# A kernel with a static order: the scheduler may now pick the engine of many operations and ranks by the following chain, and loads, stores and tables are rearranged

## The chip, the cores and the metric

The kernel runs on one core of a Trainium2 chip. The metric is the device time in microseconds (us) of one execution, and the medians below are over the executions of one kernel. On the core, TensorE (PE in the profile, with its weight loads as PEld) does the matrix products; VectorE (DVE), ScalarE (ACT) and GpSimd (POOL) do the elementwise work; SyncE (SP) issues most of the transfers.

## The reference

For 4 batches and 8 heads, with 768 steps and 40 channels per head, a recurrence (RWKV-7) updates a 40x40 state. The 8 heads' outputs, side by side, are a 768x320 matrix per batch. It is mixed by a Fourier transform over the sequence and over the model dimension, added to itself, layer-normalised and sent through an MLP.

```python
for t in range(S):                               # S = 768; per batch and head
    y[:, :, t] = einsum('bhd,bhde->bhe', r_t, state)
    Sa = einsum('bhde,bhe->bhd', state, a_t)
    state = state * w_t - einsum('bhd,bhe->bhde', Sa, b_t) + einsum('bhd,bhe->bhde', v_t, k_t)
x = y.transpose(0, 2, 1, 3).reshape(B, S, 320)
mixed = real(fft(fft(x, axis=1), axis=2))
u = x + mixed
un = (u - mean(u)) / sqrt(var(u) + 1e-6)         # per row of 320
out = u + maximum(un @ w_ch1, 0) @ w_ch2         # 320 -> 1280 -> 320
```

## The kernel before

The kernel works in 24 chunks of 128 steps, six per batch. For each chunk there is a preparation (loads, logarithms, products with the decay, transposes, masked 128x128 products) and a chain that carries the state from chunk to chunk. The last instruction of the chain is the DVE multiply that writes the chunk's output; where I give the time of "the chunk's output" it is the start of this multiply, which lasts 0.5 us. After the sixth chunk of a batch follow mixing, normalisation and MLP of that batch, and they overlap with the next batch's chunks. Only the last batch's have nothing to overlap with.

The program first lists its operations in Python, each with its engine, an assumed duration and what it reads and writes. A list scheduler then turns this into one fixed order per engine, which the chip executes in order:

```python
# class Plan, cut
def op(self, eng, occ, fn, w=(), r=(), lat=None, ...):
    o.eng, o.occ, o.fn, o.prio = eng, occ, fn, self.prio      # one engine, one assumed duration
    ...
def run(self, log=None):
    while left:
        for e in self.ENG:
            ...                                               # start time of each ready operation
            t0 = min(c[0] for c in cand)
            t, _, o = min((c for c in cand if c[0] <= t0 + self.slack), key=lambda c: (c[1], c[0]))
            ...                                               # lowest prio (= program step) first
        o.fn()                                                # emits the instruction
```

The parts that the argument touches are the masks (A, N, RV and M are the four masked products of a chunk), the layer normalisation between mixing and MLP, the store of the residual (x, to which the mix is added) and the loads of the MLP weights:

```python
# masks of A and N: on DVE, per half; of RV and M: two copies on ACT and one select on POOL
op("DVE", DVE(512), lambda ...: nc.vector.tensor_tensor(dst()[:, e], p2[e](), msk, Alu.mult), ...)
...
op("ACT", ACT(512), lambda ...: nc.scalar.copy(RV()[:, e], p2[e]()), ...)
op("POOL", 1.06, lambda: causal(RV()), w=[RV])

# layer normalisation; st holds mean and variance of three tiles of 128 rows
op("DVE", 0.12, eps, w=[st], r=[])                             # variance + 1e-6
op("POOL", 0.25, lambda st=st: nc.gpsimd.tensor_tensor(st()[:, 8:11], st()[:, 8:11], mhalf, Alu.pow), w=[st])
for ti in range(3):
    op("DVE", 0.45, lambda ...: nc.vector.tensor_scalar(
        un()[:, ti], u()[:, ti], st()[:, 2 * ti:2 * ti + 1], st()[:, 8 + ti:9 + ti],
        Alu.subtract, Alu.mult), w=[un[ti]], r=[u[ti], st])    # (u - mean) * (1/sigma), written as bf16
# then: transposes of un on PE, unT to SBUF by ACT, MLP products on PE

# residual: one store of the batch's six chunks (960 KB) after the last one
op("SP", 0.9, lambda: nc.sync.dma_start(xd().rearrange("(c t) d -> t c d", t=C), xb()), w=[xd], r=[xb], lat=6.0)
```

I call the DVE instruction that writes `un` "the normalisation". There are 24 of them: two halves of three tiles in each of four batches.

## Time and profile before

| what | before |
|---|---|
| median of three runs | 326.75 us (326.4 to 328.29) |
| span of the profiled run | 324.8 us |
| busy PE / DVE / ACT / POOL | 284.0 / 218.4 / 199.1 / 193.5 us |
| sixth output (end of the first batch's recurrence) | 91.9 us |
| last output (24th), and from it to the end | 286.75 us, 38.1 us |

From the page of the kernel before come the rows that matter of the busy tenths (40 equal slices of the span, so about 8.1 us each; a digit is the busy share in tenths, and PEclk is the granted TensorE clock in tenths of full speed), the shares of the chain that ended last by engine, and two groups. A group's columns are line, engine, operation, tiles, shapes and count, then busy us and mean ns of one, then idle time before it.

```profile
PE   6649875768899989999999999999997899978995
POOL 8947999653699744744896555657764642252100
PEclk9985999676999999999999999999999999999999
...
PE 47%; DVE 14%; ACT 6%; POOL 5%; issue 5%; DVEq 0%; ACTq 0%; POOLq 0%
...
L545 DVE TENSOR_SCALAR un_192<-u_175,sm_213 128x320 bf16<-128x320 f32 x6 | 3.4, 600 | 0.4 <-POOL sm_213 L543 0.4
L629 POOL TENSOR_SCALAR u_177<-u_177,sm_213 128x320 f32<-128x320 f32 x2 | 1.0, 530 | 0.0
```

PE is near its limit in the middle and is not in the first quarter, where its clock is also granted at 0.5 to 0.7 for some slices. The second group, L629, is a piece of the table generation on POOL: a multiply by a per-partition scalar and an addition of a constant, 530 ns.

The stretches view divides the span at the ends of the sixth and of the last output's multiply. Its columns are the stretch, its length, then the busy us of each engine with its count of instructions, the granted clock, the busy share of the DMA engines, and GB/s.

```profile
core 0: us, PE busy (x) PEld busy (x) DVE busy (x) ACT busy (x) POOL busy (x), PEclk, DMA share, GB/s
0.00:92.40 92.40, 68.29 (x979) 47.08 (x980) 65.85 (x111) 49.28 (x112) 69.86 (x111) 0.85 0.89 148
92.40:287.20 194.80, 184.41 (x2752) 136.06 (x2750) 140.46 (x287) 134.75 (x322) 117.38 (x160) 1.00 0.50 108
287.20:324.80 37.60, 31.25 (x223) 20.81 (x221) 12.11 (x33) 15.07 (x34) 6.22 (x12) 1.00 0.24 80
```

The middle keeps PE busy for 184.41 of 194.80 us, or 95%, at full clock. The head keeps it busy for 74%. A part of this is filler: where the scheduler foresees a gap on PE it emits products of a constant tile. The trace has 60 of them (18.8 us of PE, most of it in head and tail), so PE's busy times are not all useful work.

The timeline view has start us, duration us, engine, line, operation, tiles, shapes and count; in brackets stand the engine's idle time before it and what ended it. Here are the first two products with the decay on POOL, and the last batch's normalisation:

```profile
10.19 0.86 POOL L330 TENSOR_TENSOR nat_90<-in_117,rw_138 128x320 bf16<-128x320 f32 x1
20.56 0.86 POOL L330 TENSOR_TENSOR nat_91<-in_124,rw_139 128x320 bf16<-128x320 f32 x1 [3.91 <-DMA in_124<-in_b_dram]
...
298.36 0.87 POOL L543 TENSOR_TENSOR sm_215<-sm_215,mhalf 128x3 f32<-128x3 f32 x1 [3.69 <-DVE sm_215 L541]
299.37 1.13 DVE L545 TENSOR_SCALAR un_191<-u_176,sm_215 128x320 bf16<-128x320 f32 x3
299.83 0.17 PEld L557 LDWEIGHTS <-un_191 128*128 128x128 bf16 x3 [1.84 <-DVE un_191 L545]
301.62 0.65 PE L278 MATMUL ps_220<-unT_193,w1sb 128*128 128x384 bf16 x3 [0.31 <-ACT unT_193 L559]
```

### The profile page before, as it was taken

How to read it: one execution, taken by the hardware profiler on the slowest of the kernel's cores; microseconds unless marked ns; L12 is line 12 of the kernel's file. 1: busy time of each engine (PE TensorE's matmuls, PEld its weight loads, DVE VectorE, ACT ScalarE, POOL GpSimd, SP SyncE). 2: the span in 40 equal slices, each digit the busy share in tenths (PEclk: the TensorE clock that was granted, in tenths of full speed). 3: DMA queues.
4: the chain of work that ended last, by engine and by line, in shares of the span. 5: the costliest groups of instructions: out<-in, count | busy, mean ns of one | idle time of the engine just before them, and what ended most of it. 6: DMA issues, size and time to landing. Idle time of an engine off the chain costs nothing.

```text
span 324.8 us, 9858 instructions
## 1 busy us (share of the span) xinstructions
PE 284.0 (87%) x3948; PEld 203.9 (63%) x3948; DVE 218.4 (67%) x429; ACT 199.1 (61%) x468; POOL 193.5 (60%) x282
## 2 busy tenths in 40 slices
PE   6649875768899989999999999999997899978995
PEld 2438653555568765777787667767775566655663
DVE  7246799993977898675489996637769973306411
ACT  2225753477588478496767684975763895531850
POOL 8947999653699744744896555657764642252100
PEclk9985999676999999999999999999999999999999
DMA  8999999972788955456599763539300001134011
GB/s 137 189 169 185 171 167 169 177 124 42 122 202 197 156 97 89 91 109 128 162 194 183 130 110 89 107 77 242 123 4 2 0 2 64 42 141 124 0 61 63
DMA packets 161518, 37.67 MB, mean 116 GB/s; under 512 B 150656, under 2 KB 161152, under 8 KB 161472
## 3 DMA queue, kind: packets, MB, share of 16 engines
q1 hardware_dynamic: 159808, 35.40, 54.3%
q0 software_dynamic: 1664, 1.64, 3.0%
q8 instruction: 31, 0.51, 0.6%
q14 instruction: 15, 0.12, 0.1%
HBM read 30.80 MB, written 7.86 MB: 119 GB/s over the span
## 4 chain that ended last, share of the span: by engine, by line
PE 47%; DVE 14%; ACT 6%; POOL 5%; issue 5%; DVEq 0%; ACTq 0%; POOLq 0%
PE ps_219 L278 6%; PE ps_226 L278 5%; PE ps_223 L278 5%; PE ps_224 L278 4%; PE ps_220 L278 4%; PE ps_221 L278 3%; PE ps_222 L278 3%; PE ps_225 L278 3%; DVE un_191 L545 1%; PE ps_222 L294 1%; PE ps_225 L294 1%; DVE un_192 L545 1%; PE ps_221 L294 1%; PE ps_223 L294 1%; DVE pr_163 L367 1%
## 5 line engine op out<-in xcount | busy, mean ns | idle before, releaser
L278 PEld LDWEIGHTS <-w1sb 128*128 128x128 bf16 x240 | 21.5, 97 | 13.9 <-issue 1.2
L302 POOL TENSOR_SCALAR_AFFINE_SELECT pr_161<-pr_161 128x1024 bf16<-128x1024 bf16 x8 | 8.9, 1119 | 22.6 <-ACT pr_161 L431 12.0
L302 POOL TENSOR_SCALAR_AFFINE_SELECT pr_160<-pr_160 128x1024 bf16<-128x1024 bf16 x7 | 7.7, 1097 | 11.3 <-ACT pr_160 L431 10.1
L458 POOL TENSOR_TENSOR pm_173<-xb_172 128x320 bf16<-128x320 f32 x12 | 10.1, 861 | 3.2 <-DVE xb_172 L444 3.1
L458 POOL TENSOR_TENSOR pm_174<-xb_171 128x320 bf16<-128x320 f32 x12 | 10.1, 857 | 2.5 <-DVE xb_171 L444 2.4
L349 PEld LDWEIGHTS <-nat_91 128*128 128x128 bf16 x96 | 6.4, 105 | 8.2 <-POOL nat_91 L330 7.4
L302 POOL TENSOR_SCALAR_AFFINE_SELECT pr_159<-pr_159 128x1024 bf16<-128x1024 bf16 x6 | 7.3, 1214 | 6.8 <-ACT pr_159 L431 6.7
L302 POOL TENSOR_SCALAR_AFFINE_SELECT pr_164<-pr_164 128x1024 bf16<-128x1024 bf16 x7 | 7.7, 1095 | 4.6 <-ACT pr_164 L372 2.9
L349 PEld LDWEIGHTS <-nat_90 128*128 128x128 bf16 x96 | 6.1, 103 | 6.2 <-POOL nat_90 L330 5.6
L302 POOL TENSOR_SCALAR_AFFINE_SELECT pr_166<-pr_166 128x1024 bf16<-128x1024 bf16 x7 | 7.7, 1097 | 3.7 <-ACT pr_166 L372 2.4
L278 PEld LDWEIGHTS <-pm_174 128*128 128x128 bf16 x72 | 6.7, 110 | 2.6 <-POOL pm_174 L458 1.2
L260 PEld LDWEIGHTS <-ident_71 128*128 128x128 bf16 x60 | 5.4, 108 | 4.0 <-POOL ident_71 masks.py:199 2.0
L349 PEld LDWEIGHTS <-nat_92 128*128 128x128 bf16 x96 | 6.7, 109 | 1.7 <-POOL nat_92 L330 0.9
L278 PEld LDWEIGHTS <-pr_161 128*128 128x128 bf16 x136 | 5.5, 98 | 3.3 <-issue 1.4
L278 PEld LDWEIGHTS <-pr_159 128*128 128x128 bf16 x128 | 5.0, 97 | 3.7 <-POOL pr_159 L302 1.7
L294 PEld LDWEIGHTS <-kb_151 64*128 64x128 bf16 x128 | 4.3, 98 | 4.4 <-issue 3.3
L278 PEld LDWEIGHTS <-pm_173 128*128 128x128 bf16 x72 | 6.3, 108 | 0.8 <-issue 0.2
L349 PEld LDWEIGHTS <-nat_93 128*128 128x128 bf16 x96 | 6.2, 100 | 0.8 <-POOL nat_93 L330 0.5
L543 POOL TENSOR_TENSOR sm_213<-sm_213,mhalf 128x3 f32<-128x3 f32 x4 | 3.4, 853 | 5.6 <-DVE sm_213 L541 5.4
L302 POOL TENSOR_SCALAR_AFFINE_SELECT pr_163<-pr_163 128x1024 bf16<-128x1024 bf16 x5 | 5.5, 1094 | 2.0 <-ACT pr_163 L431 1.8
L278 PEld LDWEIGHTS <-pr_165 128*128 128x128 bf16 x128 | 5.3, 98 | 2.0 <-DVE pr_165 L367 0.7
L543 POOL TENSOR_TENSOR sm_215<-sm_215,mhalf 128x3 f32<-128x3 f32 x4 | 3.5, 873 | 5.1 <-DVE sm_215 L541 4.9
(1338 smaller groups left out, 1188.4 us busy)
## 6 DMA issues: line engine op xcount, KB each, us to landing
xd<-xb_172 SPq DMA_DIRECT2D x2, 960.0 KB, 4.9
xd<-xb_171 SPq DMA_DIRECT2D x2, 960.0 KB, 4.4
out_dram<-ot_210 SPq DMA_DIRECT2D x8, 160.0 KB, 1.8
out_dram<-ot_211 SPq DMA_DIRECT2D x8, 160.0 KB, 1.9
out_dram<-ot_212 SPq DMA_DIRECT2D x8, 160.0 KB, 1.8
u_178<-xd SPq DMA_DIRECT2D x6, 160.0 KB, 4.0
u_175<-xd SPq DMA_DIRECT2D x6, 160.0 KB, 4.0
u_176<-xd SPq DMA_DIRECT2D x6, 160.0 KB, 3.0
```

The source lines that it names most:

```text
L260: nc.tensor.matmul(ps.tiles[i][:, :m_], ident16, fill16[:, :m_], start=True, stop=True)
L278: nc.tensor.matmul(o, l_, r_, start=first, stop=True, skip_group_check=True)
L294: nc.tensor.matmul(ps2[e]()[:, q, :], lT[e * 64:(e + 1) * 64, q, :], rT[e * 64:(e + 1) * 64, q, :], start=(q == 0), stop=True, skip_group_ ...
L302: nc.gpsimd.affine_select(out=t_, in_=t_, compare_op=Alu.is_gt, fill=0.0, base=0, pattern=[[0, 2], [0, NP], [1, 128]], channel_multiplier=-1)
L349: nc.tensor.transpose(pt()[:, x_, q, :], nt()[:, j, 2 * q:2 * q + 2, :].rearrange("t h d -> t (h d)"), ident16)
L367: op("DVE", DVE(512), lambda dst=dst, p2=p2, e=e, msk=msk: nc.vector.tensor_tensor(dst()[:, e], p2[e](), msk, Alu.mult), w=[dst], r=[p2[e] ...
L458: op("POOL", 0.82, lambda i_=i_, f_=f_: nc.gpsimd.tensor_tensor(pm()[:, i_, c - 3], xb()[:, c - 3], xb()[:, c], f_), w=[pm[(i_, c)]], r=[x ...
L543: op("POOL", 0.25, lambda st=st: nc.gpsimd.tensor_tensor(st()[:, 8:11], st()[:, 8:11], mhalf, Alu.pow), w=[st])
L545: op("DVE", 0.45, lambda u=u, un=un, st=st, ti=ti: nc.vector.tensor_scalar(un()[:, ti], u()[:, ti], st()[:, 2 * ti:2 * ti + 1], st()[:, 8 ...
```

## The change

The intent is to use the three elementwise engines evenly and to start the recurrence sooner. The diff has about a thousand lines; this is its core.

```diff
 class Plan:
-    def op(self, eng, occ, fn, w=(), r=(), lat=None, par=False, alloc=()):
+    def op(self, alts, w=(), r=(), hold=(), par=False, skip=None, mode=0, dma=0.0, lock=()):
     # alts: {"DVE": (assumed us, emit), "POOL": (assumed us, emit), ...}
+    def levels(self, weight):
+        for o in reversed(self.ops):
+            c = min(c_ + self.LAT[e] for e, (c_, _) in o.alts.items()) + o.dma
+            o.level = c + max((s.level + self.HOP for s in o.succ), default=0.0)
+            o.prio = weight * o.prio - o.level
     # in run: the engine is picked by the earliest end
+                    for e2, (c, _) in o.alts.items():
+                        t = max(t0, free[e2])
+                        if e2 in o.lock:
+                            t = max(t, free["DVE"], free["POOL"])
+                        opts.append((t + c * (1 + (e2 in o.lock)) + self.LAT[e2], t, e2))
+                    starts[id(o)] = min(opts)
 # masks, each half by itself
+            op({"DVE": (cD(512), lambda ...: nc.vector.tensor_tensor(d_(), p2[e](), nsu_b if neg else su_b, Alu.mult)),
+                "ACT": (cA(512), plain)}, w=[dst[e]], r=[p2[e], NSU, SU])
+            op({"POOL": (0.56, lambda d_=d_: nc.gpsimd.affine_select(...))}, ..., skip=lambda whole=whole: not whole)
 # copies from PSUM: ACT or DVE; casts and products: two or three engines; relu: ACT or DVE
+        return {"ACT": (cA(n_), lambda: nc.scalar.copy(dst(), src())),
+                "DVE": (cD(n_, x_), lambda: nc.vector.tensor_copy(dst(), src()))}
 # the normalisation
-                op("DVE", 0.45, lambda ...: nc.vector.tensor_scalar(un()[:, ti], u()[:, ti], ..., Alu.subtract, Alu.mult),
+                op({"DVE": (0.3, lambda f_=norm: f_(nc.vector)), "POOL": (0.6, lambda f_=norm: f_(nc.gpsimd))},
+                   w=[un[ti]], r=[u[ti], st], lock=("DVE",))
 # residual: one store per chunk
-        op("SP", 0.9, lambda: nc.sync.dma_start(xd().rearrange("(c t) d -> t c d", t=C), xb()), ...)
+        op({"SP": (0.6, lambda: nc.sync.dma_start(xd()[c * C:(c + 1) * C], xb()[:, c]))}, w=[xd[c]], r=[xb[c]], dma=0.8)
 # weights of the MLP: not first, but once chunks 1 and 2 have come so far
-            load_weights()
+        if i == 3:
+            load_weights([sns[1]], [sns[2]])
 # tables: 11 scalings by a position where there were 16, and 4 wraps (angle to one period) of two steps where there were 6 of three;
 # one sine block is kept and the others come from it by the addition theorem (on DVE)
 # (also: input loads in the order w k a b v r; only the padding of the tiles is zeroed)
+    P.levels(0.3)
```

For the normalisation the scheduler compares two entries: 0.3 us on DVE, doubled by `lock` in the choice because DVE and POOL share a port in its model, and 0.6 us on POOL. The compiled order shows what it chose: of 192 half masks DVE does 83 and ACT 109 (96 each before), 36 casts go to ACT, and all 24 normalisations go from DVE to POOL.

## The prediction

> **What bounds the kernel now.** The stretches view and the recurrence's markers (the multiply that ends each chunk) split the 324.8 us span in three. Head, 0 to 92 us: the six chunks of the first batch, with no MLP to overlap; chunks finish 8 to 15 us apart (35, 43, 54, 69, 82, 92). PE is 49 to 90% busy per 10 us, its granted clock falls to 0.54-0.84 (20-30 and 50-80 us); DVE is 93-98% busy from 40 to 70 us. Body, 92 to 287: PE 83-100%, mostly above 93%, a chunk each 10.3 us: near PE-bound. From start-to-start spacings in the timeline I estimate 5.9 us of PE per chunk and 27 us per batch of MLP and mixing, some 250 us in all. Tail, 287 to 325: the last batch's mixing and MLP alone, chain almost all PE.
>
> **What the change does.** (1) Head. The weight DMAs (3% of 16 engines' span, about 9.7 us) no longer go first: in the timeline three input loads needed 3.6-4.2 us each only to issue, chunk 1's b arrived at 20.5 us, and POOL could start its first product only at 10.2 us though its input was there at 6.0. The table work on DVE (wraps of 0.7-1.6 us, about 16 us in all) falls to an estimated 10-13 us, on POOL from about 13 to 5-6 us. (2) Masks: each half (DVE 0.685 us, or ACT 0.595 plus a half-size POOL select) is placed by load; the whole select of 1.1 us after two ACT copies becomes about 0.56 us per half. By the compiled order DVE does 83 of 192 halves (96 before) and ACT 109; the 24 normalisations move to POOL (0.5 us each), 36 casts to ACT, 38 PSUM copies leave ACT for DVE. My sums: DVE 218 -> about 219, ACT 199 -> about 228, POOL 193 -> about 195. Matrix products are unchanged. Little work goes; waits do. (3) Tail: the store after the last chunk is 160 KB instead of 960 KB (4.5 us to land); DFT copies are split over engines. But the first mix waited for PE as well (7.3 us idle of DVE ended by PE), so only 1-3 us.
>
> **On the path.** Head: DVE plus ACT need an estimated 128 us for six chunks, two chunks of lookahead and the tables, 64 us each if shared evenly; the first batch should end near 76 us instead of 92: 12-18 us. Body: PE gaps at 110-120, 180-190 and 240-260 us shrink: 3-6 us. Tail 1-3 us.
>
> The Trainium skill (GPSIMD Engine Reference, Key points) says GPSIMD shares its SBUF interfaces with VectorE, contending with two-port modes; the trace agrees (a 128x128 DVE multiply took 3.63 us beside POOL memsets). The skill (TensorE: Matmul & The Clock Gate, Part 1) says idle PE is throttled; a denser head should show 0.9 or more.
>
> **Prediction:** 305 us, 80% range 292 to 318. Faster by over 2%: 0.93; within 2%: 0.05; slower: 0.02.
>
> **What would show it.** First batch's sixth output near 76 us; chunk 0's first product before 8 us; granted clock above 0.9 after 20 us; a chunk every 10 us after that; ACT busy about 228 us; last output to end about 36 us.
>
> **What would make it wrong.** The static order rests on assumed durations; if POOL or ACT is slower than assumed (ACT becomes the fullest elementwise engine), engines wait in order and the head gains little. If the body has more slack than I think, it falls below 292.

## More of the kernel before

The power for 1/sigma takes POOL 0.87 us. Three normalisations then take DVE 1.13 us, and the first MLP product starts at 301.62, so 3.26 us after the power started. The weight loads of the transposes wait 1.84 us of this.

## The result, and the profile after

The changed kernel takes 317.19 us (median of 4, 316.33 to 318.6), and the kernel before takes 327.52 us in the same rounds. The ratio is 0.9689, with a 95% interval of 0.9637 to 0.9742. A ratio here is the mean time of one kernel's fast runs over that of the other's fast runs of the same rounds, so it is not quite the ratio of the medians quoted. It is a gain of about 10 us where 22 were forecast.

From the page of the changed kernel come the same rows, and the group of the normalisation:

```profile
PE   4798879988989958999999678999996799994995
POOL 8999866977977799774468798665659852319300
PEclk9999778978999998999999799999999879997899
...
PE 58%; POOL 22%; DVE 9%; ACT 5%; issue 3%; DMA 1%; DVEq 0%; POOLq 0%; SPq 0%; ACTq 0%
...
L624 POOL TENSOR_SCALAR un_174<-u_166,sm_201 128x320 bf16<-128x320 f32 x6 | 8.5, 1435 | 0.2
```

POOL's share of the chain rose from 5% to 22%. Its normalisation takes 1435 ns. The forecast had 0.5 us. PE now has holes from the eleventh slice on, at the 5, the 6s, the 7s and the 4 of its row, with the clock below full in or after them. Before, the 30 slices from the eleventh on had none below 7 but the last.

The stretches of the changed kernel, again cut at the ends of the sixth and last output's multiply, with the columns as before:

```profile
0.00:68.60 68.60, 55.27 (x929) 41.14 (x933) 53.25 (x109) 51.37 (x113) 58.37 (x104) 0.92 1.00 169
68.60:272.00 203.40, 184.80 (x2742) 136.63 (x2743) 140.51 (x308) 140.84 (x322) 145.12 (x196) 0.95 0.56 115
272.00:316.90 44.90, 36.65 (x246) 24.12 (x246) 13.01 (x36) 15.36 (x32) 13.13 (x13) 0.92 0.18 59
```

The head shrank by 23.8 us. Then the middle grew by 8.6 us and the tail by 7.3 us. In the middle PE does as much (184.80 us against 184.41) in more time, at a clock of 0.95, and POOL has 27.7 us more to do.

The timeline shows the first product on POOL, and the last batch's normalisation:

```profile
6.31 0.86 POOL L388 TENSOR_TENSOR nat_87<-in_101,rw_122 128x320 bf16<-128x320 f32 x1
...
285.58 0.88 POOL L620 TENSOR_TENSOR sm_201<-sm_201,mhalf 128x3 f32<-128x3 f32 x1 [4.07 <-DVE sm_201 L619]
286.56 4.27 POOL L624 TENSOR_SCALAR un_174<-u_166,sm_201 128x320 bf16<-128x320 f32 x3
288.05 0.17 PEld L637 LDWEIGHTS <-un_174 128*128 128x128 bf16 x3 [3.08 <-POOL un_174 L624]
289.47 0.24 PEld L637 LDWEIGHTS <-un_174 128*128 128x128 bf16 x3 [1.25 <-POOL un_174 L624]
290.88 0.24 PEld L637 LDWEIGHTS <-un_174 128*128 128x128 bf16 x3 [1.18 <-POOL un_174 L624]
```

Three normalisations take 4.27 us where they took 1.13 us. The transposes of the three tiles follow them one by one, each after a wait, so the whole of the added time is passed on. The first MLP product starts at 291.95, which is 6.37 us after the power started, against 3.26 us before.

The waits view (who waited for what: us in total, times, longest us) has this as its second largest wait in the whole kernel; the transposes' own wait on the same instruction is listed apart from it, under PE:

```profile
PEld L637 <- POOL un_174 L624: 11.4, 9, 3.1
```

In the chain that ended last (start us, us, what), the normalisation is the work of the chain itself in every batch (the first half of each is shown):

```profile
114.35 4.28 POOL un_174 L624 x3
171.56 4.28 POOL un_174 L624 x3
238.59 4.28 POOL un_174 L624 x3
286.56 2.41 POOL un_174 L624 x2
289.40 1.44 POOL un_174 L624
```

In total, the normalisation is 9.2% of this chain (5.3% for one buffer and 3.9% for the other), or 29 us.

### The profile page after: what moved, and what is told of

The parts are those of the page before. It is cut to its first block, busy times and chain, and to the rows that moved or that the text cites. A ratio compares the mean times of both kernels' runs of the same rounds, so it can differ in the third digit from the quotient of the medians.

```text
span 316.9 us, 9903 instructions
## 1 busy us (share of the span) xinstructions
PE 276.7 (87%) x3914; PEld 201.9 (64%) x3919; DVE 206.8 (65%) x450; ACT 207.6 (66%) x466; POOL 216.6 (68%) x312
## 4 chain that ended last, share of the span: by engine, by line
PE 58%; POOL 22%; DVE 9%; ACT 5%; issue 3%; DMA 1%; DVEq 0%; POOLq 0%; SPq 0%; ACTq 0%
PE ps_69 L348 7%; PE ps_71 L348 6%; PE ps_66 L348 6%; PE ps_70 L348 6%; PE ps_67 L348 5%; PE ps_68 L348 5%; POOL un_174 L624 5%; PE ps_72 L348 5%; POOL un_175 L624 4%; PE ps_65 L348 3%; POOL nat_88 L388 2%; PE ps_65 L400 2%; PE ps_65 L433 1%; POOL nat_89 L388 1%; PE ps_72 L400 1%
## 5 line engine op out<-in xcount | busy, mean ns | idle before, releaser
L348 PEld LDWEIGHTS <-w1sb 128*128 128x128 bf16 x240 | 23.3, 104 | 16.7 <-issue 5.6
L433 PEld LDWEIGHTS <-nat_88 128*128 128x128 bf16 x120 | 8.0, 102 | 8.7 <-POOL nat_88 L388 5.5
L383 POOL TENSOR_SCALAR_AFFINE_SELECT m_155<-m_155 128x512 bf16<-128x512 bf16 x14 | 8.7, 632 | 4.3 <-ACT m_155 L379 4.3
L433 PEld LDWEIGHTS <-nat_89 128*128 128x128 bf16 x120 | 7.6, 99 | 5.8 <-POOL nat_89 L388 3.6
L383 POOL TENSOR_SCALAR_AFFINE_SELECT m_154<-m_154 128x512 bf16<-128x512 bf16 x12 | 7.5, 631 | 5.0 <-ACT m_154 L379 5.0
L433 PEld LDWEIGHTS <-nat_87 128*128 128x128 bf16 x120 | 8.8, 109 | 2.9 <-issue 1.3
L433 PEld LDWEIGHTS <-nat_90 128*128 128x128 bf16 x120 | 7.4, 99 | 5.1 <-POOL nat_90 L388 4.4
L637 PEld LDWEIGHTS <-un_174 128*128 128x128 bf16 x36 | 2.7, 117 | 11.4 <-POOL un_174 L624 11.4
L383 POOL TENSOR_SCALAR_AFFINE_SELECT pr_148<-pr_148 128x512 bf16<-128x512 bf16 x8 | 5.3, 663 | 6.0 <-ACT pr_148 L379 6.0
L383 POOL TENSOR_SCALAR_AFFINE_SELECT pr_152<-pr_152 128x512 bf16<-128x512 bf16 x11 | 6.9, 636 | 3.1 <-ACT pr_152 L379 3.1
L383 POOL TENSOR_SCALAR_AFFINE_SELECT pr_145<-pr_145 128x512 bf16<-128x512 bf16 x10 | 6.5, 654 | 3.7 <-ACT pr_145 L379 3.7
L400 PE MATMUL ps_65<-logw_120,ut_ones 128*128 128x320 f32 x8 | 5.0, 720 | 4.4 <-POOL sm_196 L675 4.4
L624 POOL TENSOR_SCALAR un_174<-u_166,sm_201 128x320 bf16<-128x320 f32 x6 | 8.5, 1435 | 0.2
L624 POOL TENSOR_SCALAR un_175<-u_167,sm_196 128x320 bf16<-128x320 f32 x6 | 8.5, 1433 | 0.1
L624 POOL TENSOR_SCALAR un_175<-u_165,sm_196 128x320 bf16<-128x320 f32 x6 | 8.5, 1429 | 0.1
L383 POOL TENSOR_SCALAR_AFFINE_SELECT pr_151<-pr_151 128x512 bf16<-128x512 bf16 x9 | 6.0, 669 | 3.2 <-ACT pr_151 L379 3.2
L383 POOL TENSOR_SCALAR_AFFINE_SELECT pr_149<-pr_149 128x512 bf16<-128x512 bf16 x8 | 5.0, 633 | 4.3 <-ACT pr_149 L379 4.3
L383 POOL TENSOR_SCALAR_AFFINE_SELECT pr_153<-pr_153 128x512 bf16<-128x512 bf16 x11 | 6.8, 633 | 1.7 <-ACT pr_153 L379 1.6
L383 POOL TENSOR_SCALAR_AFFINE_SELECT pr_147<-pr_147 128x512 bf16<-128x512 bf16 x8 | 5.0, 633 | 4.3 <-ACT pr_147 L379 4.3
L348 PE MATMUL ps_66<-unT_176,w1sb 128*128 128x384 bf16 x30 | 7.5, 366 | 0.0
```

Source lines behind the costliest of these rows:

```text
L348: nc.tensor.matmul(o, l_, r_, start=first, stop=True, skip_group_check=True)
L383: op({"POOL": (0.56, lambda d_=d_: nc.gpsimd.affine_select(out=d_(), in_=d_(), compare_op=Alu.is_gt, fill=0.0, base=0, pattern=[[0, NP], [ ...
L400: op({"PE": (0.6, lambda: nc.tensor.matmul(cum(), ut_ones, logw()))}, w=[cum], r=[logw, UT])
L433: nc.tensor.transpose(pt()[:, x_, q, :], nt()[:, j, 2 * q:2 * q + 2, :].rearrange("t h d -> t (h d)"), ident16)
L624: eng.tensor_scalar(un()[:, ti], u()[:, ti], st()[:, 2 * ti:2 * ti + 1], st()[:, 8 + ti:9 + ti], Alu.subtract, Alu.mult)
L637: nc.tensor.transpose(pt()[:, kt], un()[:, ti, d0:d0 + 128], ident16)
```

## The experiments

The theory was that the normalisation on POOL, slow and on the critical chain, takes away most of what the other parts gain. The main rival was that the rest of the change gives less than was thought, because the order rests on assumed durations and the body of the kernel is bound by PE; the longer normalisation would then fill time that is idle anyway. For the cause of the 1.43 us, the guess was its two per-partition scalars, with the subtraction and the bf16 output as rivals.

### The same order, with the normalisation emitted on the other engine

The scheduler is told what it was told in the change, so the order of everything else is the same. Only the instruction is emitted on DVE.

```diff
 # a_un_emit, against the changed kernel
-                op({"DVE": (0.3, lambda f_=norm: f_(nc.vector)), "POOL": (0.6, lambda f_=norm: f_(nc.gpsimd))},
+                op({"DVE": (0.3, lambda f_=norm: f_(nc.vector)), "POOL": (0.6, lambda f_=norm: f_(nc.vector))},
```

> The changed kernel with its schedule kept instruction for instruction, except that the 24 normalisations (1.43 us each on POOL in its trace) are emitted to DVE at the same place in program order. Theory 1 (the slow POOL normalisation sits between mixing and MLP and stalls PE four times, 11.4 us of weight-load waits plus about 9 us of product waits put down to it): 300 to 307 us, PE waits on the normalised tile below 3 us, the stretches 110-120, 170-180, 240-250 and 280-290 us back above 85% PE. Theory 2 (the other batch's work fills these gaps, so only the unfilled tail counts): 313 to 316 us.

The reverse is done in the kernel before: the same order, with the normalisation emitted on POOL.

```diff
 # b_un_emit, against the kernel before
-                op("DVE", 0.45, lambda ...: nc.vector.tensor_scalar(
+                op("DVE", 0.45, lambda ...: nc.gpsimd.tensor_scalar(
```

> The reverse: the kernel before, same schedule, with its 24 normalisations emitted to POOL instead of DVE. Theory 1: slower by 8 to 15 us (335 to 342 us), with PE waiting for POOL's normalised tile. Theory 2: slower by 2 to 4 us.

| kernel | median us (range) | ratio to before, 95% interval |
|---|---|---|
| changed | 317.19 (316.33 to 318.6) | 0.9689 (0.9637 to 0.9742) |
| changed, normalisation emitted on DVE | 298.89 (298.31 to 299.78) | 0.9157 (0.9103 to 0.9212) |
| before, normalisation emitted on POOL | 343.75 (340.68 to 344.92) | 1.0518 (1.0448 to 1.0588) |

The median of the kernel before in these rounds was 326.39 us. One instruction's engine is worth 18.3 us in the changed kernel (317.19 - 298.89; by the ratios it is 5.3% of the kernel before). In the kernel before it is worth 17 us. The instruction times would account for more: three instructions in a row take 4.27 us against 1.13 us, eight times, or 25 us. So most of the added time reached the end, and not all of it. Both runs moved further than the theory's ranges (300 to 307 and 335 to 342 us), away from the rival's. One sign expected in the trace came only in part: PE's weight loads still wait 4.6 us for the normalised tile, not below 3 (11.4 in the changed kernel), and of the four stretches named, 110 to 120 us stays at 80% busy.

The tile view (engine, operation, count: shortest/median/longest ns, first and last start us) has for the changed order with the normalisation on DVE

```profile
L624 DVE TENSOR_SCALAR un<-u,sm x24: 413/446/1043, 114.4 to 275.5; 128x320 bf16<-128x320 f32 x24
```

and for the old order with it on POOL

```profile
L545 POOL TENSOR_SCALAR un<-u,sm x24: 1422/1435/1441, 112.5 to 317.5; 128x320 bf16<-128x320 f32 x24
```

On POOL it takes 1.43 us in both orders, with hardly a spread. On DVE most take 0.45 us and the worst 1.04 us.

What this did to PE shows in 20 us from each batch's first normalisation. First the changed kernel's stretches, with the columns as before:

```profile
114.00:134.00 20.00, 15.38 (x155) 9.64 (x152) 8.09 (x20) 10.28 (x23) 18.46 (x21) 0.91 0.74 135
171.00:191.00 20.00, 14.42 (x203) 9.95 (x202) 11.55 (x26) 12.49 (x29) 17.96 (x21) 0.91 0.42 80
238.00:258.00 20.00, 15.15 (x177) 10.26 (x172) 10.41 (x24) 11.76 (x24) 16.46 (x17) 0.84 0.05 17
286.00:306.00 20.00, 15.66 (x93) 9.37 (x95) 4.66 (x14) 7.99 (x17) 9.83 (x8) 0.83 0.07 25
```

Then the stretches of the same order with the normalisation emitted on DVE:

```profile
114.00:134.00 20.00, 18.24 (x243) 12.61 (x241) 14.97 (x34) 13.05 (x30) 12.08 (x19) 1.00 0.80 155
166.00:186.00 20.00, 18.78 (x271) 13.00 (x267) 18.02 (x41) 15.90 (x37) 14.20 (x21) 1.00 0.65 120
228.00:248.00 20.00, 18.32 (x251) 13.02 (x248) 16.70 (x37) 13.88 (x29) 10.15 (x14) 1.00 0.08 26
270.00:290.00 20.00, 17.75 (x112) 10.91 (x115) 6.72 (x20) 11.17 (x24) 1.03 (x2) 0.91 0.07 25
```

In these 80 us POOL does 62.7 us of work in the first and 37.5 us in the second. PE runs 628 matrix instructions in the first and 877 in the second. In the first three stretches POOL is 82 to 92% busy: it also has the masks and products of the next batch's chunks, and they stand in one queue with the normalisations. In these stretches PE is also granted a lower clock, 0.83 to 0.91 against 0.91 to 1.00. The Trainium skill (TensorE: Matmul & The Clock Gate, Part 1) says that the throttled state is the default and activity releases it. These traces agree in part: the clock fell where the stalls were. A throttled default they do not show: in the first 10 us of the changed kernel the clock is given as 1.00 with PE 56% busy.

### Letting the scheduler choose with a true cost

The next kernel leaves DVE as the only entry. Its compiled order is the same as with both entries and the POOL entry set to the measured 1.43 us.

```diff
 # a_un_dve, against the changed kernel
-                op({"DVE": (0.3, lambda f_=norm: f_(nc.vector)), "POOL": (0.6, lambda f_=norm: f_(nc.gpsimd))},
+                op({"DVE": (0.3, lambda f_=norm: f_(nc.vector))},
```

> The changed kernel where the scheduler may place the normalisations on DVE only, so everything after the first batch is scheduled anew. (With POOL's cost set to the measured 1.43 us and the choice left free the schedule comes out the same, so this is also the calibrated version.) Theory 1: 298 to 306 us, like the run that only moves the emission. Theory 2: 312 to 316 us. If the two runs differ by more than 4 us, the reshuffling of the order itself is worth that much.

It took 297.81 us (297.02 to 299.07), a ratio of 0.9129 (0.9081 to 0.9177). That is 1.1 us below the emission alone, which the intervals do not separate. So the engine of the instruction was the matter, and planning with the right cost adds little to it.

### What makes it slow on POOL

This kernel times instructions alone. Its output is wrong, which doesn't matter for the time. Ten forms of the one instruction run four times each on POOL, then four times each on DVE, on 128x320 f32 inputs. POOL's last test instructions (powers and masks) still ran beside the first eight on DVE, of which three took 0.78 to 0.85 us and the others 0.43 to 0.45, so DVE is read at its fastest.

```diff
 # micro, the body of the kernel replaced
+    forms = (("subp_mulp", BF16, (m, s, Alu.subtract, Alu.mult)), ("subp_mulp_f", FP32, ...),
+             ("mulp_addp", BF16, (m, s, Alu.mult, Alu.add)), ("mulp_addi", BF16, (m, 0.3, Alu.mult, Alu.add)), ...
+             ("mulp", BF16, (m, None, Alu.mult)), ("subp", BF16, (m, None, Alu.subtract)))
+        for _ in range(4):
+            nc.gpsimd.tensor_scalar(o, x, *args)
```

> A wrong result on purpose: it only times single instructions, [128, 320] tensor_scalar forms on POOL and then on DVE. Theory: what makes the normalisation slow on POOL (1.43 us, while the table step of the same size, multiply by a per-partition scalar and add a constant, took 0.53 us) is that both scalars are read per partition; then subtract-multiply and multiply-add with two per-partition scalars take about 1.4 us and every form with at most one takes about 0.5 us. Rivals: it is the subtraction (then forms with one per-partition subtraction are slow as well), or the bf16 result (then all bf16 forms are slow). DVE: 0.3 to 0.45 us for all.

It ran once, in 60.7 us. In the names of the following groups "p" stands for a per-partition scalar and "i" for a constant, so `g_subp_mulp` is the normalisation's form on POOL and `v_` marks DVE. The columns are those of the groups above.

```profile
L181 POOL TENSOR_SCALAR g_subp_mulp__90<-x,sc 128x320 bf16<-128x320 f32 x4 | 5.7, 1431 | 0.1
L181 POOL TENSOR_SCALAR g_subi_muli__120<-x 128x320 bf16<-128x320 f32 x4 | 5.1, 1283 | 0.3
L181 POOL TENSOR_SCALAR g_mulp__130<-x,sc 128x320 bf16<-128x320 f32 x4 | 4.4, 1088 | 0.2
L181 POOL TENSOR_SCALAR g_mulp_addp__100<-x,sc 128x320 bf16<-128x320 f32 x4 | 2.4, 607 | 0.0
L181 POOL TENSOR_SCALAR g_mulp_addi__105<-x,sc 128x320 bf16<-128x320 f32 x4 | 2.1, 527 | 0.1
L196 DVE TENSOR_SCALAR v_mulp_addp__165<-gate,sc 128x320 bf16<-128x320 f32 x4 | 1.7, 434 | 0.0
L196 DVE TENSOR_SCALAR v_mulp__195<-gate,sc 128x320 bf16<-128x320 f32 x4 | 1.5, 373 | 0.0
```

The guess was wrong, and so were its rivals. Two per-partition scalars cost POOL only 0.08 us more than one and a constant (607 against 527 ns). The output type does not matter (1430 ns with an f32 output). It is not the subtraction as such either, because a multiply alone takes 1088 ns and a subtraction alone 1087 ns. Among the forms tried, a multiply followed by an addition is the only fast one on POOL: 458 to 607 ns, depending on its scalars. Subtract-then-multiply takes 1283 to 1431 ns. Why the pair is fast is not shown. On DVE all forms take 313 to 435 ns at their fastest.

This puts the error of the forecast in one place. The prediction names no source for its 0.5 us; the nearest figure in the trace before is the 530 ns of the table generation. That is a multiply-and-add, and the normalisation is a subtract-and-multiply of the same size on the same engine. The Trainium skill (GPSIMD Engine Reference, section 4.1 Engine selection) says of POOL that "1-input is roughly line-rate". The multiply-and-add comes near (607 against 434 ns). The other forms do not (1088 against 373 ns), and there the measurement decides.

### The normalisation stays on POOL in its fast form

u times 1/sigma plus (-mean times 1/sigma) is the same value. It needs one more DVE instruction of 128x3 elements per half.

```diff
 # a_muladd, against the changed kernel
+            op({"DVE": (0.2, lambda st=st: nc.vector.scalar_tensor_tensor(
+                st()[:, 11:14], st()[:, 0:5:2], -1.0, st()[:, 8:11], Alu.mult, Alu.mult))}, w=[st])
...
-                    eng.tensor_scalar(un()[:, ti], u()[:, ti], st()[:, 2 * ti:2 * ti + 1], st()[:, 8 + ti:9 + ti],
-                                      Alu.subtract, Alu.mult)
+                    eng.tensor_scalar(un()[:, ti], u()[:, ti], st()[:, 8 + ti:9 + ti], st()[:, 11 + ti:12 + ti],
+                                      Alu.mult, Alu.add)
```

> The changed kernel with its scheduler's assumed 0.6 us for the POOL normalisation made true: scale by 1/sigma and add -mean/sigma (0.607 us on POOL in the instruction timing, 1.43 for subtract-multiply), one more 128x3 DVE step per half; all 24 stay on POOL. If only the duration of the instruction is at fault: 296 to 302 us, as with DVE. If POOL is the wrong engine in itself (in-order queue behind masks and products): above 306 us.

It took 298.86 us (298.13 to 301.21), a ratio of 0.9158 (0.9104 to 0.9211). All 24 stay on POOL, as the tile view of this kernel has them:

```profile
L626 POOL TENSOR_SCALAR un<-u,sm x24: 592/612/622, 114.9 to 274.6; 128x320 bf16<-128x320 f32 x24
```

So it was not the move to POOL that cost 18 us but the form of the instruction there. At 0.61 us, close to the 0.6 us that the change's own cost table assumed, the change is worth about 28 us.

### What the other parts are worth

Each of these undoes one part, with the kernel that has the normalisation on DVE (297.81 us, ratio 0.9129) as the base. The first takes the choice away: all engines are as in the kernel before.

```diff
 # u_fixed, cut
-        return {"ACT": (cA(n_), ...copy...), "DVE": (cD(n_, x_), ...tensor_copy...)}
+        return {e_: {"ACT": ..., "DVE": ...}[e_]}            # the engine of the kernel before
-            (masks by half, DVE or ACT with a half select)
+            (A and N on DVE; RV and M two ACT copies and one whole POOL select)
-            op({"ACT": ..., "DVE": (cD(384), ...tensor_scalar_max...)}, ...)
+            op({"ACT": ...}, ...)                               # likewise products, casts, folds, reversals
```

> From the changed kernel with the normalisations on DVE (297.8 us), one part undone: the engine of every copy, cast, product and mask is fixed as in the kernel before (two masks on DVE, two on ACT with one whole POOL select). Theory A (my prediction's: free placement shortens the waits in head and body): slower by 8 to 15 us, 306 to 313 us. Theory B (the gain is from order of work, not from engines): below 302 us.

The second drops the ranking by the following chain:

```diff
 # u_prio
-    P.levels(0.3)
```

> From the same 297.8 us version, one part undone: urgency is the old step number alone, not the longest chain that follows. Theory A: slower by 3 to 8 us. Theory B (order of work is the main gain): slower by more than 12 us.

The third loads the MLP's weights at the start again:

```diff
 # u_weights
+            at(0, 80)
+            load_weights([], [])
-        if i == 3:
-            load_weights([sns[1]], [sns[2]])
```

> From the same 297.8 us version, one part undone: the MLP weights are loaded at the start, without waiting for chunks 1 and 2. Theory A (weights take some 9.7 us of all DMA engines out of the first loads and delay chunk 1): slower by 4 to 9 us, first batch's sixth output 6 us or more later. Theory B (the head is bound by DVE and ACT, the load delay is absorbed): under 2 us slower.

The fourth stores the residual once per batch again:

```diff
 # u_xd
+        op({"SP": (0.9, lambda: nc.sync.dma_start(xd().rearrange("(c t) d -> t c d", t=C), xb()))}, w=[xd], r=[xb],
+           dma=4.8)
-        keep(c, xbs[bb], xds[bb])
```

> From the 297.8 us version (changed kernel, normalisations on DVE), one part undone: the residual of a batch is stored by one 960 KB transfer after its last chunk, not chunk by chunk. The first mixing of the last batch waits for DFT products as well as for the residual, so slower by 0 to 3 us, all of it after the last chunk's output.

The fifth generates the tables as the kernel before does:

```diff
 # u_tables, cut
-        for y_, lo, hi in ((ya, 0, 768), (yb, 0, 640), (yb, 640, 1280), (yb, 1280, 1858)):   # two steps each
+        for lo in (0, 768):
+            wrap(ta, lo, lo + 768, S)                                                       # three steps each
+        wrap(tb, 0, 516, S); wrap(tb, 516, 516 + DM, DM); ...
```

> From the same 297.8 us version, one part undone: the longer table generation of the kernel before (6 wraps of three DVE steps, 20 POOL scalings, wide iotas). It adds about 5 us on DVE and 7 us on POOL in the first batch, where both are nearly full: slower by 3 to 7 us, with the sixth output later by as much. If the head's work is hidden by the rest, under 2 us.

| undone from the base | median us (range) | ratio to before, 95% interval | against the base | sixth output, us |
|---|---|---|---|---|
| nothing | 297.81 (297.02 to 299.07) | 0.9129 (0.9081 to 0.9177) | | 68.2 |
| choice of engine | 315.57 (314.02 to 316.43) | 0.9651 (0.9603 to 0.97) | +17 us | 83.6 |
| short tables | 306.09 (302.74 to 306.54) | 0.933 (0.9266 to 0.9394) | +7 us | 84.8 |
| ranking by chain | 304.8 (303.27 to 305.72) | 0.9311 (0.9258 to 0.9365) | +6 us | 72.0 |
| store per chunk | 303.11 (301.05 to 304.64) | 0.9277 (0.9222 to 0.9332) | +5 us | 70.0 |
| weights later | 301.81 (300.97 to 304.41) | 0.9249 (0.9191 to 0.9307) | +4 us | 84.3 |

The column "against the base" is the difference of the ratios times 327 us; the medians of the kernel before were 326.39, 326.75 and 327.61 us. The sum is 39 us, and the base is only 28 us ahead of the kernel before, so the parts do not add up. Against what was expected, the choice of engine (8 to 15 us) and the store (0 to 3 us) cost more; the ranking lies within its range, and tables and weights lie at the edge of theirs.

The last column also shows how little the sixth output says of the end. Weights at the start put it back by 16 us, and cost 4 us in the end. The longer tables put it back by 17 us and cost 7, where the two were expected to be alike. (The text of `u_tables` speaks of 20 scalings; the kernel before has 16.)

### A cheaper 1/sigma, and how much a mere re-weighting moves

The power on POOL takes 0.87 us and stands on the same chain before every normalisation. Two ACT instructions of 128x3 elements (logarithm, then exponential with a scale of -0.5) take 0.2 us each by the trace, and ACT has both functions loaded already. A power on DVE does not compile, so it was not run.

```diff
 # n_rstd, against the base with the normalisation on DVE
-            op({"POOL": (0.25, lambda st=st: nc.gpsimd.tensor_tensor(
-                st()[:, 8:11], st()[:, 8:11], mhalf, Alu.pow))}, w=[st], r=[MH])
+            op({"ACT": (0.1, lambda st=st: nc.scalar.activation(st()[:, 8:11], st()[:, 8:11], Act.Ln))}, w=[st])
+            op({"ACT": (0.1, lambda st=st: nc.scalar.activation(st()[:, 8:11], st()[:, 8:11], Act.Exp, scale=-0.5))},
+               w=[st])
```

> An attempt at a version that beats both: the 297.8 us version with 1/sigma made by two 128x3 steps on ACT (logarithm and exponential, whose table is loaded anyway) in place of the 0.87 us POOL power. It saves about 0.5 us on the chain of each half, of which the last batch's first half is exposed: 0 to 2 us faster than 297.8.

```diff
 # n_rstd_w5, against n_rstd
-    P.levels(0.3)
+    P.levels(0.5)
```

> The same with the step number weighing 0.5 instead of 0.3 against the longest chain that follows. No theory says which weight is best; the run without the chain lost 7 us, so between 295 and 303 us.

The first took 295.43 us (293.01 to 296.52), a ratio of 0.9016 (0.8955 to 0.9078), and gave a correct result. It is the fastest kernel, about 32 us ahead of the kernel before and 2.4 us ahead of its base by the medians, a little more than the 0 to 2 us expected. The second differs in one number of the ranking and took 302.71 us (301.24 to 303.47), a ratio of 0.9244 (0.9195 to 0.9292). It has the same work on the same chip and loses 7 us.

This sets a limit on the table above. Any edit that changes the list of operations or their ranking gives another order of all instructions, and another order alone moved the time by 7 us. Of the parts, only the choice of engines stands clearly above that, and it is measured against a single re-weighting. That the tables, the ranking, the stores and the weights each help fits their intent, but neither their signs nor their sizes are settled by these runs. A rival was not tested: none of the undone kernels got a weight of its own (those that rank by chain kept 0.3), so a part of each loss, that of the choice of engines too, may be that this weight suits their order less. By the same measure the gain of the cheaper 1/sigma (0.9129 to 0.9016) may be partly luck of the order.

## Why the prediction was wrong

The forecast was 305 us (292 to 318) against 317.19 measured. The measured time lies within the range; of the forecast gain of 22 us about 10 came.

**The step that failed** is the one that the prediction put as "the 24 normalisations move to POOL (0.5 us each)". The move was seen, and the mechanism, engines chosen by load so that waits vanish, is supported: without the choice 17 us are lost. The term was mis-sized. It measured 1.43 us each, so 22.4 us of POOL work more than costed (24 x 0.935, with 0.5 us for each). The sum for POOL was "about 195" and measured 216.6 us. In the trace before, 0.5 us is what a multiply-and-add of this size takes there. The prediction did name a POOL slower than assumed as a thing that could make it wrong, but looked for its effect in the head; it came between mixing and MLP. The 0.5 us would have been nearly right for the multiply-and-add form: with it the changed kernel measures 298.86 us, and with the normalisation on DVE 298.89 us. Both lie within the range, on the fast side of the forecast; that they lie so near it is in part luck, because the gain came at other places than forecast (see below).

**Where on the chain.** The prediction treated the move as a matter of the engines' sums. In the trace before, PE's weight loads already waited 1.84 us for three normalisations of 1.13 us, with the MLP behind them, and the page of the kernel before has `un_191` and `un_192` in the chain that ended last with 1% each. That was the sign that this work lies on the chain. In the changed kernel it is 29 us of the chain of 316.9 us, in all four batches.

Point by point:

- "First batch's sixth output near 76 us": it came at 68.2 us, so the head gained more than the 12 to 18 us said, 23.7 us by this marker. But by the end of the first batch's MLP (the start of its last final addition) only 4.3 us of it was left (156.1 against 151.8 us). With the normalisation on DVE it was 8.6 us (147.5 us). By tens of us from 70 to 100, DVE was 88 to 99% and ACT 78 to 95% busy. The first addition of a mixed tile to x, on DVE, started at 109.0 us against 107.8 us before, and the first normalisation at 114.3 against 114.2. The chunks were ahead (the tenth output at 106.5 us against 129.7), but the end of the first batch's mixing was not. That the full DVE and ACT held it back is likely and was not tested. A marker that comes earlier is not time gained at the end.
- "Chunk 0's first product before 8 us": right. It started at 6.31 us (10.19 before).
- "Granted clock above 0.9 after 20 us": wrong. It was 0.67 to 0.83 from 30 to 50 us, and 0.83 to 0.91 in the stalls. It was still 0.69 from 40 to 50 us with the normalisation on DVE, so the normalisation is not its cause there. PE was 76% busy in these 10 us; but the kernel before had 79% in the same stretch at a clock of 1.00, so the busy share alone does not explain the clock.
- "A chunk every 10 us after that": wrong as run, 11.8 us from the tenth to the last output. With the normalisation on DVE it was 10.66 us.
- "Body ... 3-6 us": it lost 8.6 us by the stretches as run. With the normalisation on DVE it gained 7.2 us from the sixth to the last output (187.7 against 194.9 us), a little more than was said. The batches' ends tell where the 27.5 us of that kernel arise: 8.6 us by the end of the first batch, and the rest between the ends of the later ones, which lie 59.3, 55.0 and 32.6 us apart against 65.0, 62.6 and 37.6 us before. The prediction had put most of the gain into the head; most of it is seen at the end only after that.
- "Matrix products are unchanged": but for the filler, which fell from 60 to 26 products.
- "a 128x128 DVE multiply took 3.63 us beside POOL memsets": in the changed kernel, where three memsets (0.1 to 0.5 us each) and an iota ran beside it, the same instruction took 0.37 us.
- "ACT busy about 228 us", "DVE about 219": 207.6 and 206.8 us. Both sums were too high, by 20 and 12 us; the lower load did not make up for POOL.
- "Last output to end about 36 us": 45.4 us, and 41.7 us with the normalisation on DVE. Part of this is no loss. In the changed order the batch before finishes its MLP about 6 us after the last output, and in the kernel before it had finished 3 us ahead of it. Work moved across the marker.

The rival, that the rest of the change gives less than thought, is refuted: without the slow form the change gives 27 to 29 us, more than the 22 forecast. What stays open is how the 28 us divide among tables, ranking, stores and weights, and why POOL is fast for one pair of operations only.

## What to carry to other kernels

Before an instruction moves to another engine, cost it from the very same form there, with the same pair of operations and the same operands, and if the trace has none, time that form by itself: the same shape on the same engine took 0.53 us for one pair and 1.43 us for another. A scheduler that picks engines is as good as its cost table, and one wrong entry (0.6 us for 1.43 us) on work between two stages took 18 of 28 us here; look first at who already waits for the work that is to move. Where a static order is computed, run a neutral re-weighting to learn how far a mere re-ordering moves the time, and don't attribute differences below that to a part of the change.

## What the Trainium skill lacked or had wrong

- GPSIMD Engine Reference, section 4.1 Engine selection: it calls 1-input work on this engine roughly line-rate. That nearly holds for multiply-then-add (527 to 607 ns on 128x320 with a per-partition scalar, against 374 to 434 ns on DVE). A plain copy, run once, took 449 ns. The statement does not hold for a single multiply (1088 against 373 ns) or for subtract-then-multiply (1283 to 1431 against 313 to 435 ns). The page has no cost by pair of operations.
- GPSIMD Engine Reference, Key points: "For elementwise work, the DVE is structurally ~2× faster." For this instruction the ratio lay between 1.4 (607 over 434 ns) and 4.1 (1283 over 313 ns), by the pair of operations. One factor misleads.
- GPSIMD Engine Reference, none of its sections: a power on 128x3 elements takes this engine 0.84 to 0.96 us, as long as a product of two 128x320 tiles (0.86 us), and more than twice the two ACT steps of 0.2 us each that replaced it.
- TensorE: Matmul & The Clock Gate, Part 1: nothing was shown to be wrong. The clock fell to 0.83 to 0.91 in the stalled 20 us stretches, and was 1.00 in three of the four without the stalls; the throttled state as the default is not seen (1.00 in the first 10 us, with PE 49% busy in the kernel before and 56% in the changed one).
